# Attention, routing and two expert layers in one kernel: attention's last events in a hand-written order, some low parts moved to VectorE, scatters that don't wait for each other

## The chip, the cores and the metric

The kernel runs on one core of one Trainium2 chip. The metric is the device time of one execution in microseconds, as the median of several runs. TensorE is called PE in the profile, VectorE DVE, ScalarE ACT, GpSimd POOL and SyncE SP; SP issues most transfers, ACT the transposing ones.

## What is computed

```python
# q, k, v: (4, 8, 576, 64) float32;  s: (4, 8, 576)
scores = (1/sqrt(64)) * q @ k.T
cum    = cumsum(max(s, 0))
bias   = min(-(cum[:, None] - cum[None, :]), 0)
attn   = softmax(where(causal, -1e9, scores + bias))
x      = attn @ v                       # as 2304 tokens x 512
# routing: logits sorted from the top; a token goes to the first expert
# that has fewer than 288 tokens
logits = x @ w_gate                     # 2304 x 8
for e in range(8):                      # 512 -> 1024 -> 512
    y[mask_e] = max(x[mask_e] @ w1[e], 0) @ w2[e]
h   = y @ w_in                          # 512 -> 2048
out = (max(h, 0) + alpha * min(h, 0)) @ w_out
```

w_in and w_out come as float64 bits and are turned into float32 on the chip.

## The kernel before

Float32 operands of the large products are split into a high and a low part, and three products (high x high, high x low, low x high) stand for one. So every operand costs a conversion (a copy by ACT or VectorE) and a subtraction for the low part (VectorE or GpSimd).

**Attention** (`attention`, L43 to L475) goes through 16 pairs of heads, each in four steps: query tiles 0 and 1, 2, 3, and the 64-row tails of both heads. The work of a step is cut into events (`qk` scores, `mins` the row maxima, `exps`, `split_hi` and `split_lo` of the exponentials, `etr` their transpose by DMA, `av` the products with v, `rd` and `norm` the normalisation, `finish` the store to `xd`, `lg` and `lt` the gate's logits). Each event has a tick, a place within it (ORDER) and a shift (SH); the list sorted by these is the order in which the instructions are issued on every engine. Scores and products of a step are four ticks apart (LAG). Of step i of a pair, VectorE makes the high parts of the exponentials (L283, L287, L288), GpSimd the low parts (L294, L297, L298), ACT issues the transposing DMA (L301), PE then multiplies (L316 to L326), and VectorE normalises (L344). The gate's logits follow: transposes by PE (L363, L383), a copy by ACT (L367, L386), products (L373, L392), a sum by VectorE (L379, L396).

The cumulated bias enters the scores as a product of two small matrices, `SB` and `MB` (L240). Their rows are loaded by `load_bias` for two pairs at a time (L116 to L119), into one of two buffers.

A `hook` called at each tick loads chunks of w_in and w_out (512 KB each) and converts them: `conv` (L671) makes float32 in three VectorE steps (L680, L681, L682) and then splits it, the high part by ACT, the low part by GpSimd (L653, L654). There are 32 chunks, two for each of 16 f-tiles of the second layer; `early_conv` takes steps of `conv` within attention, 11 chunks of which are finished there. The rest follows in the threshold search and in expert 0.

**Routing** (`Router.phase`): the threshold of each expert is found by a search over bits on VectorE and PE (`search`, L510 to L561; L523 is the comparison of all tokens with the candidates), then the expert's tokens get their places and an index list `idt` (L619). Phase 0 stands between attention and the experts, and conversion steps are issued in its waits; the phases of experts 1 to 7 run beside the experts.

**Experts** (`FFN.run`): for each expert POOL gathers its tokens by indirect DMA (L775), the first layers (`L1`, `L2` with kind 0) and then the second ones (kind 1) run f-tile by f-tile. L1's result goes through ACT (L738, L745), VectorE (L740) and GpSimd (L746 low part) to L2 (L758 to L760). At the end of an expert its rows are transposed and scattered to the output by POOL in three indirect DMAs (L831; of the last expert L788). All of these write the same output, so each waits until the one before has landed.

Of the kernel before, what the change touches and what calls it, by code (L numbers as in the profile page):

```python
# [31 lines left out]
LB=-7  # L32
# [9 lines left out]
ORDER=('pe0','pe1','pe2','pe3','dve0','dveA','dveB','act1','sp','dve2','act2','dve3','pl','act3','ld')  # L42
def attention(tc, q, k, v, s, w_gate, xd, L, C, cp, ap, psum, dp, hook=None, rawp=None):  # L43
# [5 lines left out]
    # ---- loads  # L49
# [34 lines left out]
    # ---- keeps the array's clock up until the products begin  # L84
# [4 lines left out]
    # ---- cumulative sums  # L89
# [12 lines left out]
    def init_bias(i):  # L102
        sf=SB[i].bitcast(F); mf=MB[i].bitcast(F)
        nc.gpsimd.memset(mf,0.0)
        nc.gpsimd.memset(mf[64:66],1.0)
        if i: nc.vector.memset(sf,0.0)
        for h in range(4):
            r=32*(h%2)
            for c0,n in ((512*h,512),(2048+64*h,64)):
                nc.gpsimd.memset(sf[r:r+2,c0:c0+n],-1.0)  # L110
    def load_bias(hb):
        i=hb%2
        hv=chd[4*hb:4*hb+4]
# [21 lines left out]
    # ---- q, k transposes and splits  # L135
# [82 lines left out]
    # ---- scores and softmax  # L218
    SM={}; DEN={}
    # steps of a head pair: q tiles (0, 1), 2, 3 and the 64-row tail of both heads  # L220
    PARTS={0:((0,0),(1,128)),1:((2,0),),2:((3,0),)}
    WID={0:384,1:384,2:512}
    def qk(p,i):
        hb=p//2; sb,mb=SB[hb%2],MB[hb%2][:,p%2]
        kh,kl=OPS['k',p]
        sc=[psum.tile([128,512],F,name='sc',bufs=4) for h in range(2)]
        if i<3:
            qh,ql=OPS['q',p]
            # the two heads' products lie on different rows of the array and run side by side
            for ti,off in PARTS[i]:  # L230
# [6 lines left out]
                for h in range(2):  # L237
                    c0=512*(2*(p%2)+h)+128*ti
                    nc.tensor.matmul(sc[h][:,off+N-128:off+N],idb,mk,start=False,stop=False,skip_group_check=True)
                    nc.tensor.matmul(sc[h][:,off:off+N],sb[:,c0:c0+128],mb[:,:N],start=False,stop=True)  # L240
        else:
            qt=QT[p%2]
            for h in range(2):
# [6 lines left out]
                nc.tensor.matmul(o,sb[:,2048+128*(p%2):2048+128*(p%2)+128],mb[:,ks],start=False,stop=True)  # L250
# [807 lines left out]
```

## Time and profile before

| | |
|---|---|
| median of 3 runs | 1031.24 us (1024.48 to 1032.9) |
| span of the profiled execution | 1021.2 us |
| median less that span | 10.0 us |
| PE, DVE, ACT, POOL busy | 913.3, 647.7, 456.9, 501.1 us |
| attention, until the search's first reduction | 0 to 265.6 us |
| threshold search, phase 0 | 265.6 to 299 us |
| expert 0: first layers, second layers | 312 to 350, 350 to 402 us |
| the other experts, last scatters | to 1006, to 1021.2 us |

The span is the time from the first to the last instruction of one execution that the profiler recorded; the time of a run has some microseconds around it. In a timeline row the first number is the start, the second the length; behind a group stands in brackets how long the engine was idle before it, and what ended that.

### The profile page before, as it was taken

How to read it: one execution, taken by the hardware profiler on the slowest of the kernel's cores; microseconds unless marked ns; L12 is line 12 of the kernel's file. 1: busy time of each engine (PE TensorE's matmuls, PEld its weight loads, DVE VectorE, ACT ScalarE, POOL GpSimd, SP SyncE). 2: the span in 40 equal slices, each digit the busy share in tenths (PEclk: the TensorE clock that was granted, in tenths of full speed). 3: DMA queues.
4: the chain of work that ended last, by engine and by line, in shares of the span. 5: the costliest groups of instructions: out<-in, count | busy, mean ns of one | idle time of the engine just before them, and what ended most of it. 6: DMA issues, size and time to landing. Idle time of an engine off the chain costs nothing.

```text
span 1021.2 us, 21290 instructions
## 1 busy us (share of the span) xinstructions
PE 913.3 (89%) x8043; PEld 844.5 (83%) x8043; DVE 647.7 (63%) x1413; ACT 456.9 (45%) x1234; POOL 501.1 (49%) x460
## 2 busy tenths in 40 slices
PE   6898999884438898999999999999999999999995
PEld 5677777763427788999999999999999999999994
DVE  7888888898885987856676545645654533332310
ACT  4677777753213334433334344334434444444332
POOL 6555655556244457725255355526526526535322
PEclk9899999986558999999999999999999999999998
DMA  6999999987765021313263035207205313422200
GB/s 124 210 240 212 212 223 211 260 182 130 237 224 180 16 64 52 98 36 98 61 158 84 17 73 143 52 22 173 67 8 137 102 29 88 127 53 73 45 1 24
DMA packets 269878, 116.10 MB, mean 114 GB/s; under 512 B 207504, under 2 KB 257040, under 8 KB 269776
## 3 DMA queue, kind: packets, MB, share of 16 engines
q1 hardware_dynamic: 127728, 70.56, 25.9%
q10 hardware_dynamic: 138976, 34.75, 20.0%
q0 software_dynamic: 3072, 9.44, 3.1%
q8 instruction: 63, 1.03, 0.4%
q14 instruction: 39, 0.32, 0.1%
HBM read 70.39 MB, written 9.58 MB: 78 GB/s over the span
## 4 chain that ended last, share of the span: by engine, by line
PE 49%; DVE 14%; DMA 6%; issue 6%; POOL 4%; ACT 2%; SPq 1%; POOLq 0%; DVEq 0%; ACTq 0%
PE hp L728 8%; PE acc L758 8%; PE hp L729 8%; PE hp L730 7%; PE acc L760 7%; PE acc L759 7%; DMA out_dram<-stg,idt 3%; PE mi L533 2%; DVE g L740 1%; POOL hh L746 1%; DMA et<-eh 1%; DVE a L680 1%; DVE a L682 1%; DVE a L681 1%; DMA rB<-in_moe_w_out_dram 1%
## 5 line engine op out<-in xcount | busy, mean ns | idle before, releaser
L746 POOL TENSOR_TENSOR hh<-g,hh 128x288 fp32r<-128x288 f32 x128 | 118.3, 925 | 246.3 <-ACT hh L745 214.9
L740 DVE SCALAR_TENSOR_TENSOR g<-g,nal 128x288 f32<-128x288 f32 x128 | 76.6, 599 | 162.2 <-ACT g L739 150.5
L294 POOL TENSOR_TENSOR eh<-e,eh 128x768 f16<-128x768 f32 (+1 forms) x48 | 91.1, 1899 | 69.7 <-DVE eh L283 43.3
L654 POOL TENSOR_TENSOR w0r<-wraw,w0r 128x512 fp32r<-128x512 f32 x62 | 89.6, 1445 | 58.2 <-ACT w0r L653 58.0
L738 ACT ACTIVATE g<-hp 128x288 f32<-128x288 f32 x128 | 52.3, 409 | 135.9 <-PE hp L730 121.8
L745 ACT ACTIVATE hh<-g 128x288 fp32r<-128x288 f32 x128 | 56.9, 444 | 117.9 <-DVE g L740 117.9
L758 PE MATMUL acc<-hh,rB 128*128 128x288 f32 x352 | 106.2, 302 | 0.0
L760 PE MATMUL acc<-hh,rB 128*128 128x288 f32 x352 | 104.3, 296 | 0.0
L759 PE MATMUL acc<-hh,rB 128*128 128x288 f32 x352 | 104.1, 296 | 0.0
L728 PE MATMUL hp<-x2h,rB 128*128 128x288 f32 x320 | 90.8, 305 | 0.0
L729 PE MATMUL hp<-x2h,rB 128*128 128x288 f32 x320 | 89.7, 300 | 0.5 <-POOL rB L654 0.5
L734 DVE SCALAR_TENSOR_TENSOR hh<-hp,hh 128x288 fp32r<-128x288 f32 x64 | 29.0, 453 | 84.7 <-ACT hh L733 84.7
L271 ACT ACTIVATE e<-sc,mn 128x128 f32<-128x128 f32 (+3 forms) x128 | 66.2, 528 | 34.5 <-DVE mn L261 24.7
L759 PE MATMUL acc<-hh,w1r 128*128 128x288 f32 x256 | 76.5, 299 | 0.9 <-POOL w1r L654 0.9
L758 PE MATMUL acc<-hh,w1r 128*128 128x288 f32 x256 | 77.1, 301 | 0.0
L760 PE MATMUL acc<-hh,w1r 128*128 128x288 f32 x256 | 76.1, 297 | 0.0
L728 PE MATMUL hp<-xTh,w0r 128*128 128x288 f32 x256 | 73.9, 308 | 0.9 <-ACT xTh L781 0.6
L729 PE MATMUL hp<-xTh,w0r 128*128 128x288 f32 x256 | 73.2, 305 | 0.3 <-POOL w0r L654 0.3
L758 PEld LDWEIGHTS acc<-hh,rB 128*128 128x128 f32 x352 | 66.5, 189 | 0.3
L760 PEld LDWEIGHTS acc<-hh,rB 128*128 128x128 f32 x352 | 66.5, 189 | 0.0
L654 POOL TENSOR_TENSOR w1r<-wraw,w1r 128x512 fp32r<-128x512 f32 x46 | 64.1, 1393 | 4.8 <-ACT w1r L653 4.6
L759 PEld LDWEIGHTS acc<-hh,rB 128*128 128x128 f32 x352 | 66.3, 188 | 0.0
(297 smaller groups left out, 2907.6 us busy)
## 6 DMA issues: line engine op xcount, KB each, us to landing
wraw<-in_moe_w_dram SPq DMA_DIRECT2D x128, 256.0 KB
rB<-in_moe_w_out_dram SPq DMA_DIRECT2D x11, 512.0 KB
rB<-in_moe_w_in_dram SPq DMA_DIRECT2D x10, 512.0 KB
qr<-in_q_dram SPq DMA_DIRECT2D x32, 128.0 KB
kr<-in_k_dram SPq DMA_DIRECT2D x32, 128.0 KB
vr<-in_v_dram SPq DMA_DIRECT2D x32, 128.0 KB
xd<-xm SPq DMA_DIRECT2D x16, 256.0 KB
rA<-in_moe_w_in_dram SPq DMA_DIRECT2D x3, 512.0 KB
```

Source lines behind the costliest of these rows:

```text
L271: nc.scalar.activation(e[:,h,off:off+N],sc[:,off:off+N],AF.Exp,bias=mn[:,2*z+h:2*z+h+1],scale=-1.0,accum_out=den[:,2*ti+h:2*ti+h+1])
L294: nc.gpsimd.tensor_sub(e4[:,:,1],e[:,:,:N],e4[:,:,0])
L654: lo_eng.tensor_sub(l,x,h.bitcast(F))
L728: nc.tensor.matmul(ps,wh[k],x[0][:,k],start=(k==0),stop=False)
L729: nc.tensor.matmul(ps,wl[k],x[0][:,k],start=False,stop=False)
L730: for k in range(4): nc.tensor.matmul(ps,wh[k],x[1][:,k],start=False,stop=(k==3))
L740: nc.vector.scalar_tensor_tensor(g,g2[:,1],self.nal[:,f:f+1],g,op0=OP.mult,op1=OP.add)
L745: nc.scalar.activation(hh[:,0],g,AF.Copy)
L746: nc.gpsimd.tensor_sub(hh[:,1],g,hh[:,0].bitcast(F))
L758: nc.tensor.matmul(a,wh[:,ds],hh[:,0],start=(f==0),stop=False)
L759: nc.tensor.matmul(a,wl[:,ds],hh[:,0],start=False,stop=False)
L760: nc.tensor.matmul(a,wh[:,ds],hh[:,1],start=False,stop=(f==last))
```

## The change

It has five parts.

1. The events of attention from tick 62.9 on are not sorted by tick any more but issued in the order of a written list, DRAIN. In it the low parts of steps 0 and 1 of the last pair are made by VectorE; its steps 2 and 3 are not split and transposed by DMA, but transposed by PE from the float32 exponentials (`etT`), copied by ACT into the high part (`etA`), and VectorE subtracts for the low part (`etL`). Integers in the list are conversion steps, nine in all; the two conversion steps per tick from tick 64 on are gone. Behind the list `even` finishes the chunk that is open.
2. From the list's first conversion on, `conv` makes the low part of a chunk on VectorE, behind the first step of the next chunk, no longer on GpSimd. Where the second layer of expert 0 needs a chunk that isn't converted, `L1` and `L2` take its steps on the spot. Four chunks move from attention into the search and behind it.
3. The bias is loaded per pair, into buffers half as large; the set for pair p+2 comes after pair p has used its buffer.
4. The router's pool `rp` is opened outside attention, so that it shares no memory with it.
5. A scatter doesn't wait for the scatter before; a memset of one element stands ahead of each on POOL.

```diff
+DRAIN=(('mins30',P),('mins31',P),('split_lo1',P),('av1',Q),('av3',Q),('etT20',P),('etT21',P),('etr1',P),('etA20',P),('etA21',P),('exps31',P),('lg_pe',13),
+    ('rd_4',Q),('norm_main',Q),1,('etL20',P),('etL21',P),('rd_1',P),('etT30',P),('etT31',P),('norm_tail',Q),('finish',Q),('lg_T',Q),('etA30',P),('etA31',P),
...
+    ('lt_T',3),('lt_act',3),('lg_pe',P),('lt_pe',3),('lg_dve',P),('lt_dve',3))
-    SB=[ap.tile([128,2304],R,name=f'sb{i}') for i in range(2)]
-    MB=[ap.tile([128,2,576],R,name=f'mb{i}') for i in range(2)]
+    SB=[ap.tile([128,1152],R,name=f'sb{i}') for i in range(2)]
+    MB=[ap.tile([128,576],R,name=f'mb{i}') for i in range(2)]
-    def load_bias(hb):
-        i=hb%2
-        hv=chd[4*hb:4*hb+4]
+    def load_bias(p):
+        i=p%2
+        hv=chd[2*p:2*p+2]
...
-        e=SM.pop(('e',p,i)); eh=SM['eh',p,i]
+        e=SM.pop(('e',p,i)); eh=SM['eh',p,i]; E=nc.vector if p==NP-1 else nc.gpsimd
...
+    def etT(p,i,h):
...
+            for j in range(WID[i]//128): nc.tensor.transpose(tp[:,128*j:128*j+128],e[:,h,128*j:128*j+128],idf)
+    def etA(p,i,h):
+        hi,lo,tp=et2(p,i,h)
+        nc.scalar.activation(hi,tp,AF.Copy)
+    def etL(p,i,h):
+        hi,lo,tp=et2(p,i,h); SM.pop(('tp',p,i,h))
+        nc.vector.tensor_sub(lo,tp,hi)
...
     def conv(self,c0,c1):
-        V=self.nc.vector
+        V=self.nc.vector; left=None
+        def low():
+            w,a,c=left
+            V.tensor_sub(w[:,1],a.bitcast(F),w[:,0].bitcast(F)); self.nc64=c+1
         for c in range(c0,c1):
+            if left and (self.halt or c not in self.c64):
+                low(); left=None; self.open=False; yield 1
...
+                if o==0 and left:
+                    low(); left=None; yield 1
...
-            self.split(w[:,0],w[:,1],a.bitcast(F),V if self.inM1 and c%4<CV else self.nc.gpsimd)
+            if self.late:
+                self.nc.scalar.activation(w[:,0],a.bitcast(F),AF.Copy); left=(w,a,c)
...
+    def even(self):
+        self.halt=True
+        while self.open: self.cstep(1)
+        self.halt=False
...
     def L1(self,n,kind,f):
+        while kind and self.nc64<=2*f: self.cstep(1)
...
+    def scatter(self,idt,j,t):
+        self.nc.gpsimd.memset(self.mark,0.0)
+        i=self.nc.gpsimd.indirect_dma_start(out=self.out,out_offset=bass.IndirectOffsetOnAxis(ap=idt[:,j:j+1],axis=0),in_=t,in_offset=None)
+        self.tc.declare_no_dep(i.ins,group='out',reason='rows of different tokens')
+        self.tc.add_to_no_dep_group('out',i.ins)
...
-                if TE0 <= t < TE1:
-                    ffn.early_conv(EC2)
+            ffn.even()
```

VectorE's instructions at the very end of attention, before the change (L680 to L682 are conversion steps, `qr`, `kr`, `vr` the places of chunks, `a` the chunk in work, `L` the logits, `tp` their product):

```order
L680 TENSOR_SCALAR a_4447<-kr 128x512
L681 SCALAR_TENSOR_TENSOR a_4447<-kr,a_4447 128x512
L682 SCALAR_TENSOR_TENSOR a_4447<-kr,a_4447 128x512
L379 TENSOR_TENSOR L<-L,tp 128x32
L680 TENSOR_SCALAR a_4458<-vr 128x512
L681 SCALAR_TENSOR_TENSOR a_4458<-vr,a_4458 128x512
L682 SCALAR_TENSOR_TENSOR a_4458<-vr,a_4458 128x512
L396 COPY L<-tp 64x8
L379 TENSOR_TENSOR L<-L,tp 128x32
```

and after it (L734 to L736 are the conversion steps, L723 a low part, L375 the normalisation, L410 and L427 the logits):

```order
L410 TENSOR_TENSOR L<-L,tp 128x32
L375 SCALAR_TENSOR_TENSOR xm<-av,vcc,rd 128x512
L410 TENSOR_TENSOR L<-L,tp 128x32
L736 SCALAR_TENSOR_TENSOR a_4415<-qr,a_4415 128x512
L734 TENSOR_SCALAR a_4459<-kr 128x512
L723 TENSOR_TENSOR qr<-a_4415,qr 128x512
L410 TENSOR_TENSOR L<-L,tp 128x32
L427 COPY L<-tp 64x8
L735 SCALAR_TENSOR_TENSOR a_4459<-kr,a_4459 128x512
L736 SCALAR_TENSOR_TENSOR a_4459<-kr,a_4459 128x512
L723 TENSOR_TENSOR kr<-a_4459,kr 128x512
```

The conversion went three steps at a time ahead of the logits; now single steps stand between the other work, low parts among them, and behind the last logits (L427) `even` adds two steps and a low part.

VectorE in the threshold search, before (L523 compares the tokens' values with the candidates, L529, L535, L551 and L553 make the next candidates, L680 to L682 are conversion steps):

```order
L523 TENSOR_TENSOR A<-mm,w_4573 128x279 x2
L529 SCALAR_TENSOR_TENSOR w_4597<-ci,w_4573 128x32
L680 TENSOR_SCALAR a_4602<-rB 128x512
L535 TENSOR_SCALAR wf<-mi 31x8
L681 SCALAR_TENSOR_TENSOR a_4602<-rB,a_4602 128x512
L551 TENSOR_REDUCE dig<-mi 128x1
L553 TENSOR_TENSOR w_4597<-w_4597,dig 128x32
L523 TENSOR_TENSOR A<-mm,w_4597 128x279 x2
L529 SCALAR_TENSOR_TENSOR w_4634<-ci,w_4597 128x32
L682 SCALAR_TENSOR_TENSOR a_4602<-rB,a_4602 128x512
```

and after (L570, L576, L582, L598, L600 are those lines, L734 to L736 the conversion, L723 a low part):

```order
L570 TENSOR_TENSOR A<-mm,w_4586 128x279 x2
L576 SCALAR_TENSOR_TENSOR w_4610<-ci,w_4586 128x32
L734 TENSOR_SCALAR a_4614<-qr 128x512
L723 TENSOR_TENSOR vr<-a_4571,vr 128x512
L582 TENSOR_SCALAR wf<-mi 31x8
L735 SCALAR_TENSOR_TENSOR a_4614<-qr,a_4614 128x512
L598 TENSOR_REDUCE dig<-mi 128x1
L600 TENSOR_TENSOR w_4610<-w_4610,dig 128x32
L570 TENSOR_TENSOR A<-mm,w_4610 128x279 x2
L576 SCALAR_TENSOR_TENSOR w_4647<-ci,w_4610 128x32
L736 SCALAR_TENSOR_TENSOR a_4614<-qr,a_4614 128x512
```

There are as many conversion steps between the comparisons as before, on chunks that are four earlier in the row, and one low part per chunk has come in.

POOL at the end of the program, before (L746 is the low part of the second layer's hidden rows, L831 and L788 are the scatters):

```order
L831 DMA out_dram<-stg,idt 2304x512
L746 TENSOR_TENSOR hh<-g,hh 128x288 x16
L788 DMA out_dram<-stg,idt 2304x512 x2
L788 DMA out_dram<-a_13823,idt 2304x512
```

and after (L811 is that low part, L857 the memset, L858 the scatter):

```order
L857 MEMSET mark 1x1
L858 DMA out_dram<-stg,idt 2304x512
L811 TENSOR_TENSOR hh<-g,hh 128x288 x16
L857 MEMSET mark 1x1
L858 DMA out_dram<-stg,idt 2304x512
L857 MEMSET mark 1x1
L858 DMA out_dram<-stg,idt 2304x512
L857 MEMSET mark 1x1
L858 DMA out_dram<-a_13887,idt 2304x512
```

The scatters are as many as before, with a memset ahead of each.

## Rows read from the trace of the kernel before

**Rows 1.** Busy time by engine in three stretches (columns: stretch, length, busy us of PE, PEld, DVE, ACT, POOL, clock, DMA share, GB/s).

```profile
265.00:299.00 34.00, 8.16 (x156) 6.59 (x157) 31.49 (x95) 5.04 (x8) 8.45 (x6) 0.50 0.79 271
...
325.00:350.00 25.00, 20.28 (x182) 18.73 (x180) 24.66 (x39) 9.43 (x21) 17.00 (x10) 1.00 0.10 26
350.00:400.00 50.00, 48.22 (x404) 46.31 (x405) 40.07 (x80) 20.87 (x52) 27.67 (x25) 1.00 0.18 51
```

**Rows 2.** Timeline of TensorE at attention's end (start us, us, line, operation).

```profile
252.41 0.23 PE L316 MATMUL av<-vhl,et 128*128 128x64 f16 x1 [9.18 <-DMA et<-eh]
...
255.62 0.29 PE L322 MATMUL tp<-vhl,et 128*128 128x128 f16 x1 [0.79 <-DMA et<-eh]
...
259.06 1.09 PE L363 MATMUL tp<-cf,xm 128*128 128x128 f32 x4
...
261.70 1.72 PE L373 MATMUL tp<-wg,xT 128*128 128x8 f32 x8
263.26 1.85 PE L392 MATMUL tp<-wgt,zt 128*128 128x8 f32 x8
```

**Rows 3.** Timeline of GpSimd: a gather of expert 0, two scatters of the last expert.

```profile
300.52 1.36 POOL L775 DMA_INDIRECT stg<-xd,idt  x1 [0.31 <-issue]
...
1011.98 0.92 POOL L788 DMA_INDIRECT out_dram<-stg,idt  x1 [2.62 <-DMA out_dram<-stg,idt]
1015.51 0.92 POOL L788 DMA_INDIRECT out_dram<-a,idt  x1 [2.61 <-DMA out_dram<-stg,idt]
```

**Rows 4.** Timeline of ACT and its queue (ACTq) at attention's end.

```profile
240.70 0.20 ACT L275 ACTIVATION_READ_ACCUMULATOR e<-sc,mn 128x1 f32 x1
...
246.11 4.19 ACTq L301 DMA_TRANSPOSE et<-eh  x1
...
250.43 1.29 ACTq L301 DMA_TRANSPOSE et<-eh  x1
```

**Rows 5.** Timeline of VectorE at attention's end: a normalisation, two steps of a conversion.

```profile
254.87 0.75 DVE L344 SCALAR_TENSOR_TENSOR xm<-av,vcc,rd 128x512 f32<-128x512 f32 x1 [2.74 <-PE av L318]
255.54 0.41 DVE L680 TENSOR_SCALAR a<-qr 128x512 int32<-128x512 int32 x1
255.99 0.69 DVE L681 SCALAR_TENSOR_TENSOR a<-qr,a 128x512 int32<-128x512 int32 x1
```

**Rows 6.** Timeline of VectorE in the threshold search and just behind it.

```profile
271.24 1.82 DVE L523 TENSOR_TENSOR A<-mm,w 128x279 bf16<-128x279 f32 x2
...
274.64 0.81 DVE L523 TENSOR_TENSOR A<-mm,w 128x279 bf16<-128x279 f32 x2
...
300.40 0.69 DVE L654 TENSOR_TENSOR w1r<-wraw,w1r 128x512 fp32r<-128x512 f32 x1
```

**Rows 7.** Timeline of GpSimd in the threshold search.

```profile
271.13 1.26 POOL L654 TENSOR_TENSOR rB<-a,rB 128x512 fp32r<-128x512 f32 x1 [6.53 <-DMA rB<-in_moe_w_out_dram]
```

**Rows 8.** Timeline of VectorE in expert 0's second layers.

```profile
357.54 1.55 DVE L740 SCALAR_TENSOR_TENSOR g<-g,nal 128x288 f32<-128x288 f32 x1
```

**Rows 9.** Timeline of GpSimd in expert 0's second layers.

```profile
353.26 0.80 POOL L746 TENSOR_TENSOR hh<-g,hh 128x288 fp32r<-128x288 f32 x1 [4.19 <-ACT hh L745]
355.71 1.82 POOL L746 TENSOR_TENSOR hh<-g,hh 128x288 fp32r<-128x288 f32 x1 [1.65 <-ACT hh L745]
357.50 1.28 POOL L654 TENSOR_TENSOR rB<-a,rB 128x512 fp32r<-128x512 f32 x1
```

**Rows 10.** Waits of the whole run (engine, line, what for; us, times, longest).

```profile
POOL out_dram L831 <- DMA out_dram<-stg,idt: 19.7, 7, 3.5
...
PE acc L760 <- POOL hh L746: 2.2, 2, 1.2
```

**Rows 11.** Timeline of VectorE at the start.

```profile
1.32 1.98 DVE L79 MEMSET sb<- 128x2304 f32 x1 [0.45 <-issue]
```

**Rows 12.** Timeline of SP's queue in attention.

```profile
110.74 0.37 SPq L355 DMA_DIRECT2D xd<-xm  x1
```

**Rows 13.** Timeline of TensorE: the first use of the bias by pair 8.

```profile
120.78 0.31 PE L240 MATMUL sc<-mb,sb 128*128 128x128 f32 x1
```

More of the change, by code (lines that the diff above doesn't have):

```diff
@@ L299, in etr, with et2 @@
     def etr(p,i):
-        et=ap.tile([128,(9 if i==3 else WID[i]//32),128],H,name=f'et{i}',bufs=2)
-        (nc.scalar if TQ else nc.sync).dma_start_transpose(et,SM.pop(('eh',p,i)))
+        et=ap.tile([128,(10 if i==3 else WID[i]//32),128],H,name=f'et{i}',bufs=2)
+        (nc.scalar if TQ else nc.sync).dma_start_transpose(et[:,0:9] if i==3 else et,SM.pop(('eh',p,i)))
         SM['T',p,i]=et
+    def etT(p,i,h):
+        e=SM['e',p,i]; ev=e.rearrange("p a b -> p (a b)")
+        if h==0: SM['T',p,i]=ap.tile([128,(10 if i==3 else WID[i]//32),128],H,name=f'et{i}',bufs=2)
+        else: SM.pop(('e',p,i)); SM.pop(('mn',p,i))
+        tp=SM['tp',p,i,h]=psum.tile([128,512],F,name='sc',bufs=4)
+        if i==3:
+            if h==0:
+                for j in range(4): nc.tensor.transpose(tp[:,128*j:128*j+128],ev[:,128*j:128*j+128],idf)
+            else: nc.tensor.transpose(tp[0:64,0:128],ev[:,512:576],idf)
+        else:
+            for j in range(WID[i]//128): nc.tensor.transpose(tp[:,128*j:128*j+128],e[:,h,128*j:128*j+128],idf)
+    def et2(p,i,h):
+        et=SM['T',p,i]; tp=SM['tp',p,i,h]
+        if i==3:
+            if h==0: return et[:,0:4,:],et[:,4:8,:],tp.rearrange("p (j q) -> p j q",j=4)
+            return et[0:64,8,:],et[0:64,9,:],tp[0:64,0:128]
+        e4=et.rearrange("p (h t j) q -> p h t (j q)",h=2,t=2)
+        return e4[:,h,0],e4[:,h,1],tp[:,0:WID[i]]
+    def etA(p,i,h):
[4 more added lines that the diff above has]
+        nc.vector.tensor_sub(lo,tp,hi)
     AV={}; XM={}; XT={}
@@ L427, in attention @@
     for z in range(2): at(V0[2]+1+z,'act3',v3_act,0,z); at(V0[2]+2+z,'dve2',v3_dve,0,z)
+    for p in range(1,NP): at(4*p+LB,'ld',load_bias,p)
     for p in range(1,NP): T_events(p,4*(p-1)+(TP1 if p==1 else 0))
@@ L459, in attention @@
     ev.sort(key=lambda e:e[0])
-    tmin=int(ev[0][0]//1); tmax=int(ev[-1][0]//1)
-    for t in range(tmin,tmax+1):
+    tmin=int(ev[0][0]//1)
+    drain=[e for e in ev if e[0]>=END]; ev=[e for e in ev if e[0]<END]
+    named={(key(f,a),a[0]):(f,a) for _,f,a in drain}
+    P=NP-1
+    for x in [(etT,P,2,0),(etT,P,2,1),(etA,P,2,0),(etA,P,2,1),(etL,P,2,0),(etL,P,2,1),(etT,P,3,0),(etT,P,3,1),(etA,P,3,0),(etA,P,3,1),(etL,P,3,0),(etL,P,3,1)]:
+        named[x[0].__name__+str(x[2])+str(x[3]),P]=(x[0],x[1:])
+    for x in DRAIN:
+        if isinstance(x,int): ev.append((END,hook,(-1,x)))
+        else:
+            f,a=named.pop(x); ev.append((END,f,a))
+    left=set(x[0] for x in named)
+    assert left<={'split_hi2','split_lo2','split_hi3','split_lo3','etr2','etr3'},named.keys()
+    t=tmin
+    while ev:
         while ev and ev[0][0]<t+1:
@@ L464, in attention @@
         if t==TI: init_bias(1)
-        if hook: hook(t,tmax+1)
+        hook(t,0)
+        t+=1
+    while t<END+10:
+        hook(t,0); t+=1
 NT,NE,CAP=18,8,288
@@ L641, in __init__ @@
         self.steps=0; self.l2done=0; self.inM1=False; self.gd=GDL; self.fine=False
-        self.cg=self.conv(0,2*ND); self.nl=0; self.nc64=0
+        self.cg=self.conv(0,2*ND); self.nl=0; self.nc64=0; self.late=self.halt=self.open=False
     def alphas(self,alpha):
@@ L748, in L2 @@
     def L2(self,n,kind,f):
+        while kind and self.nc64<=2*f+1: self.cstep(1)
         nc=self.nc
@@ L787, in ot @@
         nc.scalar.activation(t,ps[0:96,:],AF.Copy)
-        nc.gpsimd.indirect_dma_start(out=self.out,out_offset=bass.IndirectOffsetOnAxis(ap=idt[:,j:j+1],axis=0),in_=t,in_offset=None)
+        self.scatter(idt,j,t)
+    def scatter(self,idt,j,t):
[3 more added lines that the diff above has]
+        self.tc.add_to_no_dep_group('out',i.ins)
     def planes(self): return self.fp.tile([128,512],I,name='a64',bufs=PB).bitcast(U16)
@@ L830, in Y, with Z @@
             V.tensor_copy(t[j].bitcast(U16).rearrange("p (e z) -> p z e",z=2),b[j][0:96].rearrange("p (z e) -> p z e",z=2))
-        def Z(j): nc.gpsimd.indirect_dma_start(out=self.out,out_offset=bass.IndirectOffsetOnAxis(ap=idt[:,j:j+1],axis=0),in_=t[j],in_offset=None)
+        def Z(j): self.scatter(idt,j,t[j])
         return self.relay(A,T,Y,Z,OW)
@@ L1004, in hook @@
             def hook(t, n):
+                if t < 0:
+                    if n: ffn.late = True; ffn.early_conv(n)
+                    return
                 if t == 2:
```

49 lines of the change are left out of this document (27 added, 22 removed).

## The prediction

> **What bounds the kernel now.** I read the stretches first, then the end of attention engine by engine, then the waits. Four places decide. From expert 0's second layers on TensorE is the bound: it is busy 48.22 of 50 us from 350 to 400 [rows 1]; an edit counts there only if TensorE waits for it. Before that come three places where TensorE is idle. At attention's end the reader is to see TensorE waiting 9.18 us for a transpose by DMA and then running short steps one behind another to 265.1 [rows 2]. In the first threshold search (265 to 299) VectorE is busy 31.49 of 34 us [rows 1], so it sets that stage; it nearly sets the first layers of expert 0 too (24.66 of 25 us). After the last product three scatters run one after another, each waiting 2.61 or 2.62 us for the one before to land [rows 3].
>
> **Attention's end.** Today VectorE casts the exponentials, GpSimd makes their low parts, ACT issues the transposing DMA and TensorE waits for it. The exponentials of the last step are ready at 240.9 and its transpose is issued at 250.43; the one of step 2 is issued at 246.11, holds its queue 4.19 us, and what TensorE waits for comes at 252.41 [rows 2, 4]. Behind that are the products of steps 1 and 2 (2.4 us, until VectorE's normalisation, which waits for them, starts at 254.87 [rows 5]), of step 3 (255.62 to 257.3) and the gate's chain to 265.1 [rows 2].
>
> After the change steps 2 and 3 of the last pair are transposed by TensorE straight from the float32 exponentials. TensorE's chain from 240.9: five 128x128 float32 transposes, 1.4 (four of this kind take 1.09); the transpose for the gate of pair 14, 1.1; products of step 0, 1.0 (half of the 2.4 less a bit), of steps 1 and 2, 2.4; gate product of pair 14, 0.9 (half of the eight in 1.72); products of step 3, 1.7; transpose for pair 15, 1.1; a copy by ACT, 0.7 (at most the 1.55 between the end of today's transposes, 259.06 + 1.09, and the next gate product at 261.70); its gate product, 0.9; the tail's, 1.85. That is 13.0, so 253.9 [rows 2, 4]. Then VectorE copies the tail's logits (0.2) and finishes the open conversion chunk, which now stands ahead of the search: two steps of 0.69 [rows 5] and a low part of 0.60, in all 2.0. The search starts at 256.1 instead of 265.6: **9.5 us less**. The step that VectorE takes over, lows of steps 0 to 3, lies in what it had for three of the four conversion chunks now moved out (each 0.41 + 0.69 + 0.69 = 1.79 [rows 5]). Bounds: 6.5, if the transposes and copies run at twice their price and VectorE is late by as much; 12.5, if TensorE is ready earlier, since VectorE has no conversion ahead of the last minima any more.
>
> **Threshold search.** It has as many conversion steps as before. Six low parts move from GpSimd to VectorE. On GpSimd each of them held up VectorE: the selection beside one took 1.82, the same shape without one 0.81 [rows 6], while GpSimd's subtraction (1.26, [rows 7]) ran. Six such stretches of 1.0 to 1.1 are 6.4 us. On VectorE a low part takes 0.69, 0.60 from start to start [rows 6]: six are 3.6. Difference 2.8; some of the idle 2.5 us [rows 1] is filled already, so I take **2.5 less** (0.5 to 5).
>
> **Expert 0, first layers.** Four low parts leave GpSimd, about 1.0 each of stretching, and cost 0.6 each on VectorE: 1.6, **1.5 less** (0 to 4), since VectorE is busy nearly all of the stretch.
>
> **Expert 0, second layers (350 to 402).** Here the moved conversion lands. VectorE gets four chunks more (4 x 1.79 = 7.2) and 14 low parts (8.4): 15.6 on 40.07 of 50 us [rows 1]. GpSimd loses nine subtractions, up to 1.05 of stretching each (9.4): in [rows 8, 9] a VectorE operation beginning with one (1.28) takes 1.55 and ends just behind it. So VectorE comes to 46 to 55.7 of 50, while TensorE has only 1.8 us to spare. I take **3 more** (-2 to +8). The same thing can happen to GpSimd: its product took 1.82 at 355.71 against 0.80 at 353.26 [rows 9]. The Trainium skill, "SBUF — State Buffer", section "SBUF: two separate sides", says that the two engines share a pair of ports by an exclusive lock for the whole of an instruction, which a VectorE operation with two inputs in SBUF also takes against a GpSimd one that reads SBUF; the 1.82 and the 1.55 agree. By that rule every low part on VectorE would hold GpSimd for its whole length, 14 x 0.6 = 8.4 us, and this term would be near +8 (rival B).
>
> **Scatters.** A scatter no longer waits for the one before; a one-element memset stands ahead of each. In the middle the waits are 19.7 us in seven places, but GpSimd is mostly ahead of need; TensorE is late by them twice, 2.2 in all [rows 10]: **2 less** (0 to 3.5). At the end the pitch was 3.53; without the wait it is between 1.23 (0.92 and the 0.31 between issues) and the gather's 1.67 [rows 3]. Twice the difference is 3.7 to 4.6: **4.1 less** (3.5 to 5.2; the memset, of one element, is inside that); the last one's landing stays behind it.
>
> **Start and bias.** A memset of 1.98 is halved and lies ahead of others of its engine [rows 11]: **0.5 less** (0 to 1). The bias rows are loaded per pair, 16 sets of four small DMAs on SP rather than eight, into buffers half as large; each set may only start when the pair two before has used its buffer. Room: the set for a pair can go behind the store of a row block, e.g. at 110.74, and its first use is at 120.78, 10.0 us later [rows 12, 13]. Hidden, I take 0; rival A is the other end.
>
> **Sum.** -9.5 -2.5 -1.5 +3 -2 -4.1 -0.5 = -17.1 on the profiled span of 1021.2: 1004.1. The median of the runs, 1031.24, lies 10.0 above that span; with the same 10.0 the forecast is **1014 us**. With all terms at their lower ends it would be 998, at their upper ends 1029; half way to either is 1006 and 1021, and a median of three runs that lie up to 8.4 apart adds some 3 on both sides: 1003 to 1024.
>
> **Rivals.**
> A, slower: the bias comes too late. Each set is now issued at most 10 us ahead of its use, behind SP's other loads, and the products of 13 pairs wait for it in order, with everything behind them on TensorE. From 1.34 us per pair the gain of 17 is gone; from 2.1 on the kernel is slower by 1%; at 2.5, 13 x 2.5 = 32.5, it is 1046. For it: any load of q, k or v may stand on SP ahead of a set, and the set's own four issues go one after another. Against it: 10.0 us of lead hold four issues (the store's takes 0.37 [rows 12]) and a landing as long as the transposes' 6.3 us (246.11 to 252.41).
>
> B, the saved time is given back in expert 0: VectorE at 55.7 of 50 us, with low parts that now hold up GpSimd. For it: GpSimd's 1.82 at 355.71 [rows 9], and 14 x 0.6 = 8.4 of such holds at the most. Against it: nine subtractions of 1.28 leave GpSimd (11.5), more than the holds bring. Then the term is +8 to +12 rather than +3, and the time 1019 to 1023; I put it at 1021.
>
> C, the end stays gated. Steps 0 and 1 of the last pair still go by DMA, and on ACT their issues stand ahead of the copies and the last exponentials. If one holds the queue 4.19 us, as at 246.11, and lands 6.3 after its issue (252.41), or if VectorE's conversions set the end, the gain there is 3 to 4 rather than 9.5: 1020.
>
> **How the numbers follow.** Forecast 0.70, A 0.08, B 0.12, C 0.10. Within 1% is 1020.9 to 1041.6 (about what a measurement of this kernel can tell from no change). Of the forecast's 0.70 all but 0.02 is faster by over 1%; of B and C about 0.09; so faster 0.77, within 1% 0.16, slower 0.07. The range reaches from 1003 past B and C to 1026 and leaves out A and the forecast's edges.
>
> **What would show it.** In the changed profile the search's first reduction should start near 256, with no TensorE wait over 3 us for a DMA between 240 and 254; the search should last 2 to 3 us less (no selection of 279 columns above 1.2 us); expert 0's second layer should be 1 to 5 us longer, with VectorE over 46 of 50 us; the last scatter should start about 7 us after the last product's end rather than 11. First products of a pair waiting for the bias would make it wrong, as would a TensorE gap for converted weights at expert 0.

## The result and the profile after

The changed kernel takes 1017.12 us (1015.22 to 1018.05, 4 runs) against 1032.07 for the kernel before in the same comparison: a ratio of 0.9868, 95% interval 0.9828 to 0.9907. The profiled execution has a span of 1013.2 us, 8.1 (before rounding) under the 1021.2 of the profile before. That the medians differ by 15 and the two spans by 8 is part of what follows.

The span falls into the same stages in every run of this study. Their borders are rows of the timelines: the last pair's minima (VectorE's `mn<-mn`, the sixteenth), the search's first reduction (`m<-L`), the index list (`idt<-il`), the first product of expert 0, of its second layer and of expert 1, and the end of the last product.

| stage, us | before | changed | forecast of the difference | difference |
|---|---|---|---|---|
| attention to the last minima | 239.6 | 243.7 | -0.5 | +4.1 |
| last minima to the search | 26.0 | 18.0 | -9.5 | -8.1 |
| search to the index list | 32.7 | 29.1 | -2.5 | -3.6 |
| index list to expert 0's first product | 13.8 | 16.2 | none | +2.3 |
| expert 0, first layers | 35.3 | 33.8 | -1.5 | -1.5 |
| expert 0, second layers, to expert 1 | 62.2 | 72.0 | +3 | +9.8 |
| experts 1 to 7 | 597.1 | 590.6 | -2 | -6.5 |
| last product to the end | 14.5 | 9.9 | -4.1 | -4.6 |
| span | 1021.2 | 1013.2 | -17.1 | -8.1 |

At attention's end, TensorE's timeline of the changed kernel answers to [rows 2]:

```profile
242.82 0.23 PE L350 MATMUL tp<-vhl,et 128*128 128x128 f16 x1 [2.14 <-DMA et<-eh]
...
243.81 1.09 PE L317 MATMUL sc<-cf,e 128*128 128x128 f32 x8
...
247.90 0.92 PE L314 MATMUL sc<-cf,e 128*128 128x128 f32 x4 [2.21 <-ACT e L278]
```

The 9.18 us for a transposing DMA are gone. The longest waits are 2.14 for the last DMA that is left and 2.21 for the last exponentials. ACT's timeline, which answers to [rows 4], shows why these are late:

```profile
244.78 1.46 ACTq L304 DMA_TRANSPOSE et<-eh  x1
246.28 1.09 ACT L327 ACTIVATE et<-sc 128x512 f16<-128x512 f32 x2 [3.60 <-DVE a L734]
247.25 0.50 ACT L278 ACTIVATE e<-sc,mn 128x288 f32<-128x288 f32 x1
```

Their minima were ready at 243.9, but the issue of step 1's transpose stands ahead of them and waited until VectorE had made that step's low part. VectorE's timeline, for [rows 5 and 6]:

```profile
258.67 0.17 DVE L427 COPY L<-tp 64x8 f32<-64x8 f32 x1 [0.60 <-PE tp L423]
258.87 0.69 DVE L735 SCALAR_TENSOR_TENSOR a<-kr,a 128x512 int32<-128x512 int32 x1
259.59 0.69 DVE L736 SCALAR_TENSOR_TENSOR a<-kr,a 128x512 int32<-128x512 int32 x1
260.98 0.69 DVE L723 TENSOR_TENSOR kr<-a,kr 128x512 fp32r<-128x512 f32 x1 [0.69 <-ACT kr L742]
...
266.87 0.81 DVE L570 TENSOR_TENSOR A<-mm,w 128x279 bf16<-128x279 f32 x2
...
268.03 0.69 DVE L723 TENSOR_TENSOR vr<-a,vr 128x512 fp32r<-128x512 f32 x1
```

Behind the last logits (258.67) `even` takes 2.8 us, as its low part waits 0.69 for ACT's copy. In the search the selection that took 1.82 beside GpSimd takes 0.81 again, and a low part on VectorE takes 0.69, as in [rows 6].

Expert 0's second layers, by windows that span them in the kernel before and in the changed one (columns as in [rows 1]):

```profile
347.50:409.60 62.10, 56.15 (x450) 53.58 (x450) 50.21 (x91) 26.09 (x65) 36.97 (x32) 0.97 0.17 49
```

```profile
340.70:412.70 72.00, 61.80 (x451) 58.17 (x450) 60.27 (x119) 29.61 (x72) 25.86 (x23) 0.91 0.15 46
```

TensorE does the same products, but is busy for 5.7 us more, at a granted clock of 0.91 instead of 0.97, and idle for 4.2 us more. Its waits there (us in all, times, longest), first in the kernel before, then in the changed one:

```profile
PE mi L779 <- DMA stg<-xd,idt: 2.4, 1, 2.4
PE mi L613 <- DVE rb L609: 1.2, 1, 1.2
...
PE hp L729 <- POOL rB L654: 0.5, 1, 0.5
```

```profile
PE hp L793 <- ACT rB L742: 3.6, 2, 1.9
PE mi L660 <- DVE rb L656: 2.4, 1, 2.4
PE hp L794 <- DVE rB L723: 1.7, 2, 1.2
```

`rB` are converted chunks, the high part by ACT and the low part by VectorE: weights that come too late. `rb` is a step of expert 1's routing on VectorE. The timeline of TensorE shows when it waits, and the windows at which clock it ran:

```profile
375.22 0.62 PE L660 MATMUL mi<-rb,A 128*32 128x18 bf16 x18 [2.40 <-DVE rb L656]
...
398.12 0.40 PE L793 MATMUL hp<-x2h,rB 128*128 128x288 f32 x1 [1.71 <-ACT rB L742]
...
406.55 0.40 PE L793 MATMUL hp<-x2h,rB 128*128 128x288 f32 x1 [1.93 <-ACT rB L742]
```

```profile
345.00:350.00 5.00, 5.00 (x27) 4.71 (x28) 2.51 (x8) 2.23 (x5) 1.14 (x2) 0.70 0.00 0
370.00:375.00 5.00, 2.81 (x22) 2.67 (x21) 4.86 (x13) 1.67 (x4) 1.61 (x2) 1.00 0.83 256
375.00:380.00 5.00, 4.78 (x40) 4.76 (x40) 3.81 (x12) 1.67 (x4) 0.94 (x2) 0.66 0.02 5
390.00:395.00 5.00, 4.43 (x33) 3.96 (x32) 4.96 (x4) 2.48 (x7) 4.77 (x4) 1.00 0.21 57
395.00:400.00 5.00, 2.78 (x15) 2.34 (x16) 4.24 (x8) 1.94 (x5) 2.00 (x2) 0.92 0.17 51
400.00:405.00 5.00, 4.61 (x28) 4.42 (x27) 4.31 (x7) 2.08 (x5) 2.26 (x2) 0.74 0.14 39
405.00:412.70 7.70, 4.99 (x24) 4.77 (x25) 5.60 (x9) 4.12 (x9) 3.46 (x3) 0.79 0.20 68
```

So the surplus does not come from late chunks alone. Counted from the first product of the stretch, the same product comes 1.6 us later than in the kernel before after 16 us, 4.3 us later after 44 us, and 9.4 us later in the last chunk but one. The first 4.3 us arise before TensorE waits for any chunk: in a spell at a lower clock from 345 on, whose cause the profile does not show, and in the routing wait with the lower clock behind it. The rest comes with the two late chunks and the lower clock behind them. Ahead of the routing wait and of the first wait for a chunk VectorE is nearly full (4.86 us of the 5 from 370, 4.96 of the 5 from 390).

And GpSimd at the end, for [rows 3]:

```profile
1004.99 0.92 POOL L858 DMA_INDIRECT out_dram<-stg,idt  x1 [3.66 <-ACT stg L853]
1005.91 0.09 POOL L857 MEMSET mark<- 1x1 f32 x1
1006.22 0.92 POOL L858 DMA_INDIRECT out_dram<-stg,idt  x1 [0.22 <-ACT a L853]
1007.13 0.09 POOL L857 MEMSET mark<- 1x1 f32 x1
1007.44 0.92 POOL L858 DMA_INDIRECT out_dram<-a,idt  x1 [0.21 <-issue]
```

Three scatters at a pitch of 1.23 us instead of 3.53: 2 x 2.3 = 4.6 us.

One wait lies where the prediction did not look. At the start TensorE waits 6.71 us for the bias of pair 1, whose set SP issued at 28.00, three microseconds after TensorE had come to that product:

```profile
31.45 0.45 PE L243 MATMUL sc<-mb,sb 128*128 128x128 f32 x1 [6.71 <-DMA sb<-chd]
```

### The profile page after: what moved, and what is told of

Read it like the earlier page. It is cut to its first block, busy times and chain, and to the rows that moved or that the text cites. A ratio compares the mean times of both kernels' runs of the same rounds, so it can differ in the third digit from the quotient of the medians.

```text
span 1013.2 us, 21310 instructions
## 1 busy us (share of the span) xinstructions
PE 915.9 (90%) x8057; PEld 846.2 (84%) x8057; DVE 643.2 (63%) x1444; ACT 458.6 (45%) x1238; POOL 451.5 (45%) x443
## 4 chain that ended last, share of the span: by engine, by line
PE 52%; DVE 11%; DMA 3%; issue 2%; ACT 2%; POOL 1%; POOLq 0%; DVEq 0%; ACTq 0%
PE hp L793 9%; PE acc L824 8%; PE hp L795 8%; PE hp L794 8%; PE acc L826 8%; PE acc L825 8%; PE mi L580 2%; DMA a<-a 1%; DVE a L736 1%; DVE rB L723 1%; DVE a L735 1%; DVE g L805 1%; DMA stg<-xd,idt 1%; DVE A L570 1%; DMA out_dram<-stg,idt 1%
## 5 line engine op out<-in xcount | busy, mean ns | idle before, releaser
L811 POOL TENSOR_TENSOR hh<-g,hh 128x288 fp32r<-128x288 f32 x128 | 119.4, 933 | 273.9 <-ACT hh L810 264.6
L297 POOL TENSOR_TENSOR eh<-e,eh 128x768 f16<-128x768 f32 (+1 forms) x45 | 85.1, 1891 | 72.2 <-DVE eh L286 46.3
L824 PE MATMUL acc<-hh,rB 128*128 128x288 f32 x352 | 107.5, 305 | 0.0
L826 PE MATMUL acc<-hh,rB 128*128 128x288 f32 x352 | 105.5, 300 | 0.6 <-POOL hh L811 0.6
L825 PE MATMUL acc<-hh,rB 128*128 128x288 f32 x352 | 105.3, 299 | 0.0
L793 PE MATMUL hp<-xTh,w0r 128*128 128x288 f32 x256 | 72.2, 304 | 0.8 <-ACT xTh L847 0.6
L794 PE MATMUL hp<-xTh,w0r 128*128 128x288 f32 x256 | 70.7, 297 | 0.4 <-POOL w0r L702 0.4
L264 DVE TENSOR_REDUCE mn<-sc 128x1 f32<-128x128 f32 (+3 forms) x128 | 55.7, 479 | 20.8 <-PE sc L243 20.8
L826 PEld LDWEIGHTS acc<-hh,rB 128*128 128x128 f32 x352 | 67.6, 192 | 1.0 <-POOL hh L811 1.0
L824 PEld LDWEIGHTS acc<-hh,rB 128*128 128x128 f32 x352 | 67.5, 192 | 0.3
L825 PEld LDWEIGHTS acc<-hh,rB 128*128 128x128 f32 x352 | 67.4, 192 | 0.0
```

The lines of the kernel that those rows point to most:

```text
L297: E.tensor_sub(e4[:,:,1],e[:,:,:N],e4[:,:,0])
L793: nc.tensor.matmul(ps,wh[k],x[0][:,k],start=(k==0),stop=False)
L794: nc.tensor.matmul(ps,wl[k],x[0][:,k],start=False,stop=False)
L811: nc.gpsimd.tensor_sub(hh[:,1],g,hh[:,0].bitcast(F))
L824: nc.tensor.matmul(a,wh[:,ds],hh[:,0],start=(f==0),stop=False)
L825: nc.tensor.matmul(a,wl[:,ds],hh[:,0],start=False,stop=False)
```

## Experiments

The theory after the result: attention's end and the search give about what was forecast, expert 0 takes it back because the chunks that were moved there come late for TensorE, and the scatters carry the rest. Its rivals: the place of the low parts is what costs in expert 0, or the routing; the gain of experts 1 to 7 is not the scatters'. Open beside them: whether the bias is what delays attention.

### The bias of pair 1 issued early

```diff
-    for p in range(1,NP): at(4*p+LB,'ld',load_bias,p)
+    for p in range(2,NP): at(4*p+LB,'ld',load_bias,p)
-        if t==TI: init_bias(1)
+        if t==TI: init_bias(1); load_bias(1)
```

> The changed kernel with one edit: the bias set of pair 1 is issued as soon as its buffer is prepared, some 6 us earlier on SP than in the changed kernel (28.0 us there, with the first product of pair 1 waiting 6.71 us for it). Theory (attention lost its 4.2 us at the last minima to that one wait): the wait falls to under 1 us, the last minima of the last pair come near 239.5 instead of 243.72, the search starts near 257.5, the whole run is 3 to 6 us shorter than the changed kernel. Rival (attention is bound by its other engines and the wait was only one of several lags): the wait goes, but the last minima move by under 1.5 us and the run by under 2.

Measured: 1021.5 us, ratio 0.9895 (0.9834 to 0.9957). The wait fell from 6.71 to 1.92, pair 1's minima came at 38.1 instead of 42.9, but a wait of 2.69 for pair 2's bias followed, and by the last minima (247.3) nothing was left:

```profile
24.97 0.30 PE L243 MATMUL sc<-mb,sb 128*128 128x128 f32 x1 [1.92 <-DMA sb<-chd]
...
41.41 0.30 PE L243 MATMUL sc<-mb,sb 128*128 128x128 f32 x1 [2.69 <-DMA sb<-chd]
```

The theory falls: the wait at pair 1 is real, but cutting it brings nothing at attention's end. Of the rival the mechanism fits, its numbers don't: the last minima came 3.6 us later, not within 1.5, and the median is 4.4 us above the changed kernel's, though the intervals of the two ratios overlap. The rows show the clock's price beside it: this product takes 0.30 us here, at a granted clock of 1.00, and 0.45 at 31.45 in the changed kernel, where TensorE had idled for 6.71 us and the clock was at 0.50 (28 to 37 us).

### The scatters dependent again

```diff
-        self.nc.gpsimd.memset(self.mark,0.0)
         i=self.nc.gpsimd.indirect_dma_start(...)
-        self.tc.declare_no_dep(i.ins,group='out',reason='rows of different tokens')
-        self.tc.add_to_no_dep_group('out',i.ins)
```

> The changed kernel with part 5 undone: each scatter waits again for the one before, no memset. Theory (the scatters give 4.6 us at the end and most of the 6.5 us that experts 1 to 7 gain): end 4 to 5 us later behind the last product, and the last product 3 to 6 us later counted from the start of expert 1; in all 8 to 11 us longer than the changed kernel. Rival (the gain of experts 1 to 7 comes from the clock or from work that was late in expert 0): only the 4 to 5 us at the end and at most 2 before, in all 4 to 7.

Measured: 1027.61 us, ratio 0.9946 (0.991 to 0.9983), 10.5 us more than the changed kernel's median; its interval and the changed kernel's (0.9828 to 0.9907) do not meet. The end behind the last product takes 14.4 instead of 9.9, experts 1 to 7 take 594.1 instead of 590.6: 8.0 of the 13.8 us between the two profiles. Most of the other 5.8 is attention, which came to 249.5 in this profile. The theory holds. The 4.5 us at the end are plain, as every profile with free scatters has 9.9 to 10.1 there; the 3.5 in the middle are less so, as that stage varies from 589.0 to 593.7 over the other kernels that keep the change's free scatters. GpSimd's waits show the cause:

```profile
POOL out_dram L857 <- DMA out_dram<-stg,idt: 18.6, 7, 3.3
```

In the changed kernel no scatter waits for another; there they wait for the rows that they write:

```profile
POOL out_dram L858 <- DVE stg L902: 22.1, 13, 3.0
```

### Low parts on GpSimd in expert 0's second layers

```diff
     def L1(self,n,kind,f):
+        if kind: self.late=False
```

> The changed kernel with the low parts of converted chunks back on GpSimd from expert 0's second layer on (VectorE keeps them before). In the changed kernel expert 0 from its second layer to expert 1's first product takes 72.0 us against 62.1 before. Theory (VectorE with 15.6 us more is what is late there, TensorE waiting for converted chunks): 8 us leave VectorE, some 3 to 5 come back as stretching beside GpSimd, so that stretch gets 3 to 6 us shorter. Rival (the lock: GpSimd's subtractions of 1.3 hold VectorE as long as VectorE's own of 0.6 did, or longer): no change or up to 4 us longer. Second rival (the four chunks that are converted on the spot set it, wherever the low parts are made): within 2 us.

Measured: 1016.66 us, ratio 0.9854 (0.9789 to 0.9918); the stretch takes 72.8 instead of 72.0. VectorE loses little (58.74 us busy against 60.27) and TensorE waits for the same weights, now in GpSimd's name:

```profile
PE hp L795 <- POOL rB L702: 2.9, 2, 2.0
PE hp L794 <- ACT rB L701: 2.7, 2, 2.1
```

The theory falls in its numbers. The +0.8 fits both rivals: of the 8 us of low parts that left VectorE 6.5 came back as stretching beside GpSimd (its 16 operations `g<-g,nal` alone take 13.8 us instead of 9.2), and the chunks are as late as before. This run doesn't tell the two apart, and they don't exclude each other. A later one, which takes conversion steps themselves out of the stretch, shows that the moved conversion is the cost, wherever its low parts are made.

### The last exponentials ahead of the transpose's issue

```diff
-('etT21',P),('etr1',P),('etA20',P),('etA21',P),('exps31',P),
+('etT21',P),('exps31',P),('etr1',P),('etA20',P),('etA21',P),
```

> The changed kernel with one entry moved in the list: the last exponentials stand ahead of the issue of step 1's transpose and of the copies on ACT. In the changed kernel they start at 247.25, 3.5 us behind their minima, and TensorE waits 2.21 us for them. Theory (the issue, held until VectorE's low part and 1.46 us long, keeps ACT): they start within 0.5 us of their minima, TensorE's last transposes come some 2 us earlier and the search 1.5 to 2.5 us earlier. Rival (the transpose of step 1, or VectorE's list, sets the end anyway): search start within 0.7 us of the changed kernel's distance from the last minima, 18.0 us.

Measured: 1017.22 us, ratio 0.9859 (0.9794 to 0.9924). The exponentials start 0.26 us behind their minima, as the theory has it:

```profile
248.91 0.50 ACT L278 ACTIVATE e<-sc,mn 128x288 f32<-128x288 f32 x1 [1.30 <-DVE mn L267]
```

From the last minima to the search it is 17.0 instead of 18.0. The 1.0 us lies between the two expectations. Of the kernels with the written list, those without this edit lie between 16.8 and 18.8 on that stage, those with it at 16.8, 17.0, 17.2 and 19.4, so its worth stays open.

### Conversion steps in the gap before expert 0

```diff
-NX = 5
+NX = 10
-NX0 = 0
-NX1 = 0
+NX0 = 4
+NX1 = 2
```

> The changed kernel with eleven more conversion steps issued between the search and expert 0's first layer, where VectorE idles while the gathers land (13 us of idle time in the changed kernel between 296.8 and 315). Theory (expert 0's second layer loses its 9 to 10 us because chunks are converted on the spot; nearly three chunks are taken off it): that stretch, from expert 0's second layer to expert 1's first product, 72.0 us in the changed kernel, gets 5 to 8 us shorter and the run 4 to 8. Rival (what is late there is the routing of expert 1 and its gathers, or the clock): within 2 us.

Measured: 1016.31 us (1010.25 to 1018.09), ratio 0.9827 (0.9741 to 0.9914). The stretch falls from 72.0 to 60.9, further than the theory had it, and TensorE's clock there is 0.97 again:

```profile
353.10:414.00 60.90, 55.52 (x449) 53.75 (x450) 51.80 (x104) 27.04 (x67) 24.42 (x22) 0.97 0.19 53
```

VectorE is busy for 51.80 us there instead of 60.27, and TensorE's waits for converted weights fall from 5.3 to 2.2 us in all. With eleven steps off, the lag of 1.6 us after 16 us, the one of 4.3 after 44 us and the one in the last chunk but one are all gone (under 1 us each against the kernel before). The wait for the routing's step falls with them, from 2.4 to 1.5 us, so the routing was no cause of its own. The conversion that was moved into this stretch is what costs expert 0's second layers their ten microseconds: for the stage the theory holds. For the run, which was to get 4 to 8 us shorter, it doesn't. The first layers take 37.8 instead of 33.8, with the clock at half for the first 5 us of them:

```profile
315.00:320.00 5.00, 4.62 (x19) 4.62 (x20) 1.12 (x3) 1.25 (x3) 0.33 (x1) 0.50 0.36 122
```

and attention came to 252.1 in this profile, 8.4 us later than in the changed kernel's, with the same instructions. The net gain of 7 us in expert 0 does not show in the time beyond its interval.

### Three edits together

The three edits above (steps in the gap, exponentials, early bias).

> The eleven steps, the last exponentials ahead of the transpose's issue, and the early bias set of pair 1 together. If they add up: 4 to 8 from the first, 1 from the second and nothing from the third (its early gain of 4.7 us at pair 1 was gone by pair 10): 5 to 9 us under the changed kernel. If the third counts after all when the rest is earlier, up to 12.

Measured: 1015.59 us, ratio 0.9848 (0.9767 to 0.9929). Expert 0's layers take 37.6 and 63.2, the last stage before the search 17.2; attention came to 249.8. The sum of 5 to 9 us is not seen in the time.

### The kernel before with free scatters alone

> The kernel before with part 5 alone, scatters that don't wait for each other. Theory (part 5 gives 4.5 at the end and 3.5 in experts 1 to 7, in the changed kernel undone 8): span from the last product to the end 9.9 instead of 14.5; expert 1's first product to the last product 593 to 594 instead of 597.1; the run 7 to 10 us shorter than before. Second theory (waiting scatters are also what spreads the times of the kernel before from 1024 to 1039): the runs lie within 5 us of each other. Rival (the scatters count only at the end): 4 to 5 us shorter, spread as before.

Measured: 1019.04 us (1014.95 to 1027.17), ratio 0.989 (0.9795 to 0.9986). By stage the profile differs from that of before by 4.6 us at the end (9.9 against 14.5) and 2.1 in experts 1 to 7 (595.0); everything ahead agrees within 0.7. By the medians it is 11 us in this comparison and 13 against the 1032.07 of the first, most of what the whole change brings, but the interval of the ratio allows 1 to 21. The runs lie 12 us apart, so the second theory, that the waiting scatters spread the times, falls.

### The kernel before once more

> The kernel before as it is, for a second profile. Theory (the profile that the prediction rests on was one of the fastest executions: its span of 1021.2 lies 2 us under a time of about 1023, where the median is 1032): this one has a span of 1025 to 1035, and the difference lies in attention, whose last minima come 3 to 8 us after 239.6. Rival (the surplus of 10 us lies around the span): a span of 1020 to 1023.

Measured: a time of 1038.82 and a span of 1037.0. The theory holds, by more than it allowed: the profile that the prediction was made from was one of the shortest executions. Of the 15.8 us between the two spans attention has 7.1 (last minima at 246.7), the stage behind it 1.8, experts 1 to 7 4.5 (601.6). The time lies 1.8 above the span, not 10.

### The bias as before, with and without the moved pool

The first run undoes part 3 (bias rows for two pairs, buffers of twice the size), the second parts 3 and 4. The diff is what the second undoes beyond the first:

```diff
-        rp = c.enter_context(tc.tile_pool(name="rp", bufs=1))
         ep = c.enter_context(tc.tile_pool(name="ep", bufs=1))
...
             ffn.even()
         with ExitStack() as a:
+            rp = a.enter_context(tc.tile_pool(name="rp", bufs=1))
```

> The changed kernel with part 3 undone: the bias for two pairs at a time, in the buffers of before. Seen so far at the last minima of attention: 239.6, 246.7 and 239.7 us in three profiles with the old bias, 243.7, 249.5, 246.7, 248.7 and 252.1 in five with the new one. Theory (16 sets instead of eight, and the wait at pair 1, cost attention some 6 us): last minima at 236 to 244, pair 1 at 37 instead of 43, the run 4 to 8 us shorter than the changed kernel. Rival (attention differs from execution to execution by that much, or another part sets it): last minima at 244 to 252, the run within 2 us.

> Parts 3 and 4 undone: as the run before, and the router's pool opened behind attention again. Theory (part 4 counts for nothing): attention and the time as with part 3 alone undone, within 2 us. Rival (the pool's place changes attention's memory and so its waits): last minima or the search start over 3 us apart from that run's.

Measured: 1024.73 (1021.44 to 1026.63, 10 runs), ratio 0.9948 (0.9912 to 0.9984), with the last minima at 256.3; and 1013.47 (1009.45 to 1019.09, 4 runs), ratio 0.9848 (0.9749 to 0.9946), with the last minima at 246.2. For the first run neither theory nor rival held, for the second the rival did: its last minima lie over 3 us from the first run's. The old bias does not speed up attention by itself. The place of the pool changes no instruction of attention and no order, and yet the last minima lie 10 us apart in these two profiles, and every run of the one takes longer than every run of the other. The fourth combination, the new bias with the pool inside, was not run. TensorE's granted clock in the two, from 24 to 60, 60 to 120 and 120 to 190 us:

```profile
24.00:60.00 36.00, 30.77 (x302) 23.24 (x300) 28.20 (x65) 21.28 (x70) 19.00 (x18) 0.86 1.21 202
60.00:120.00 60.00, 52.98 (x553) 42.37 (x553) 43.46 (x107) 37.51 (x128) 28.12 (x27) 0.86 1.07 183
120.00:190.00 70.00, 65.55 (x773) 52.53 (x771) 61.68 (x151) 50.55 (x173) 40.97 (x35) 1.00 1.18 210
```

```profile
24.00:60.00 36.00, 31.20 (x307) 23.60 (x306) 29.04 (x68) 21.68 (x72) 18.65 (x16) 0.87 1.17 204
60.00:120.00 60.00, 55.90 (x597) 45.23 (x596) 48.13 (x119) 40.04 (x138) 31.78 (x29) 0.89 1.02 202
120.00:190.00 70.00, 65.78 (x781) 52.71 (x779) 61.82 (x153) 52.60 (x180) 41.24 (x38) 1.00 1.12 216
```

From 60 to 120 the first has the lower clock, fewer instructions done and a higher share of DMA time. Why the place of the pool should do that, no run here tells.

### Part 3 undone with the other edits

Part 3 undone, the exponentials first, and eleven steps in the gap; then seven steps instead of eleven.

> Part 3 undone, the last exponentials ahead of the transpose's issue, and the eleven conversion steps in the gap before expert 0. If the three add up (4 to 8, 1, and the 7 that the steps took off expert 0): 1003 to 1009 us. If part 3 counts for nothing: 1012 to 1016.

> As the run before with seven steps in the gap rather than eleven (with eleven, expert 0's first layer took 37.7 us instead of 33.8, the clock staying at half until 320). If the steps behind the first two gathers are what lengthens that layer: 34 to 36 us there, expert 0's second layer 63 to 66, the run within 3 us of the one with eleven. If not, it is 2 to 4 us slower.

Measured: 1020.58 (ratio 0.9908, 0.9861 to 0.9955), outside both ranges that were named, and 1022.32 (0.9953, 0.9916 to 0.999), with last minima at 251.8 and 254.3, first layers of 37.6 and 36.2 and second layers of 64.1 and 66.8. The steps do in expert 0 what they did before; attention takes it back, as with part 3 alone undone. With seven steps the first and the second layers both lie just over the ranges that were named: fewer steps shift time from the one to the other and gain nothing.

No kernel tried is shown to be faster than the changed one: the intervals of the fastest (parts 3 and 4 undone, 0.9749 to 0.9946; steps in the gap, 0.9741 to 0.9914) hold that of the changed kernel. Steps in the gap together with parts 3 and 4 undone were not tried.

## Why the prediction was right, and where its steps were not

The time of 1017 lies 3 us above the forecast, the range holds it, and the direction was right. By its steps it was less right than by its sum, and two signs came that it had named as making it wrong: a first product that waits for the bias (6.71 us, at pair 1) and a TensorE gap for converted weights in expert 0 (5.3 us in all).

- **Attention's end**: 9.5 forecast, 8.1 measured, inside 6.5 to 12.5. TensorE's chain runs as worked out; what was left out is that ACT's issue of step 1's transpose holds the last exponentials (247.25, where 240.9 was taken over from before), and that `even` takes 2.8 rather than 2.0, because its low part waits for ACT. Rival C named that issue; it cost little of the term, 1.0 us by the run that moves the exponentials, and that is within the spread of this stage.
- **Search**: 2.5 forecast, 3.6 measured. All six stretches went and nothing came in their place: VectorE is busy for 27.27 us of the 29.0, where it was busy for 30.44 of 32.7. First layers of expert 0: 1.5 and 1.5.
- **Expert 0, second layers**: +3 forecast with an end at +8, +9.8 measured: the step that failed, by its size. It is rival B that came, inside its +8 to +12, but by another way than the one it named: TensorE hardly waits for the products that GpSimd was to be held up in (0.6 us for `hh`), it waits for converted chunks and for the routing's step on VectorE. With eleven steps taken off, the surplus goes (60.9). The sum was made from VectorE's busy time between 350 and 400. The stretch in fact runs from 347.5 to 409.6 in the kernel before, not to 402; over all of it VectorE was busy for 50.21 of 62.1 us, and in the changed kernel for 60.27 of 72. Its load thus rose by 10.1 us, inside the 6 to 15.6 that were counted, and it still had idle time. What the sum missed is when the work is due: where TensorE waits, VectorE is full just before. TensorE is idle for 4.2 us more in all, and its granted clock is lowered in four spells where the kernel before has one, so that the same products take 5.7 us longer. That second part was in no term. Three of the spells come behind the waits shown above, the first behind none of them; why it came is not shown. With the low parts on GpSimd, VectorE's busy time falls by 1.5 us rather than the 8 that left it. The Trainium skill ("SBUF — State Buffer", section "SBUF: two separate sides") says that the two engines share a pair of ports by an exclusive lock, which one of them holds for a whole instruction. The trace agrees: the 6.5 us came back as stretching.
- **Gap before expert 0**: no term, +2.3 measured. The search ends 7.6 us earlier, and the first products of the gathered rows wait for gathers that land among loads which did not move with it: from 291 to 307 the DMA engines are 0.93 busy. That these loads hold the gathers was not tested.
- **Scatters**: 4.1 forecast and 4.6 measured at the end. In the middle 2 was forecast, and the runs have 3.5 (undone in the changed kernel) and 2.1 (made in the kernel before), on a stage that varies by as much; so this term is not shown to be off. The other microseconds that experts 1 to 7 gained (6.5 in all) have no shown cause.
- **Bias**: 0 taken, with rival A as the other end. Rival A's mechanism is there at pair 1 (6.71 us), a pair that the sum didn't look at: it took the room from pair 8. What it costs in the end stays open. Against the first profile of the kernel before the minima are 5.6 us late at pair 1 and still 4.1 at the last pair; but with the wait cut to 1.92 the last minima came no earlier (247.3), and a second profile of the kernel before, without any such wait, has them at 246.7.
- **The 10.0 us around the span**: wrong. The time lies 1.7 to 2.2 above the span in every run whose span is on record. The other 8 were the difference between a short profiled execution and the usual one. So the sum was off (-17.1 forecast, -8.1 between the two profiles) and the offset was off (10.0 taken, 3.9 between the changed kernel's span and its median), and in 1014 the two nearly cancel. That the time came within 3 us is luck to that extent. Against the usual execution the change is worth 15.

So the answer to where the expected gain went: the order of attention's end, the search and the first layers bring 13.2 us, and expert 0's second layers and the gap take back 12.1. Most of what stays is the scatters', as the kernel before with them alone shows (0.989 against 0.9868, within each other's intervals). Not all of it: with the scatters dependent again the rest of the change still has a ratio of 0.9946, some 5.6 us under the kernel before, and the interval (0.991 to 0.9983) leaves out 1. Which of the other parts these are, the runs don't single out.

## What to carry to other kernels

Work that is taken off a critical stretch has to go somewhere: before counting the gain, ask at what moment its result is needed in the new place, not only whether the engine there has room. A transfer that waits for an earlier one into the same output, though their rows never meet, stalls everything queued behind it on its engine; freeing it was worth about as much as attention's new end (8.0 against 8.1 us by stage). And one profile of a kernel whose runs lie 15 us apart is one draw: compare stages over several profiles before an offset or a few microseconds of one stage go into a sum.

## What the runs showed that was not expected

Attention's length varies by 17 us over these kernels, and by 8 us with the same instructions in the same order up to there:

| bias, pool | last minima, us, one profile each |
|---|---|
| old bias, pool inside | 239.6, 246.7, 239.7, 246.2 |
| new bias, pool outside | 243.7, 249.5, 246.7, 248.7, 252.1 |
| new bias, pair 1 early, pool outside | 247.3, 249.8 |
| old bias, pool outside | 256.3, 251.8, 254.3 |

Of the late ones all but one show a granted clock under full speed between 60 and 120 us (0.86 to 0.94, against 1.00 in the three profiles with the earliest minima). The exception is the second profile of the kernel before: 1.00 there, last minima at 246.7, and 0.79 from 205 us on, where the first profile of that kernel has 0.87. At half clock the same product takes 0.45 us instead of 0.30, so a short wait can grow before it is caught up; that the clock is what makes the difference, and not only goes with it, was not shown. Nor is it known why the place of a pool that attention does not use should shift it by some 10 us. As long as that is open, half of this change's worth can be won or lost in attention by an edit that has nothing to do with it.
